# Gated linear attention and a bilinear feed-forward on one core: the values term of chunks 2 to 5 in 128x32 tiles, tokens ordered at y's eviction, and a new order of the whole program

## The chip, the core and the metric

The kernel runs on one core of one Trainium2 chip. The metric is the device time of one execution in microseconds. Of a core's engines five appear here: TensorE (PE, with PEld for its weight loads), VectorE (DVE), ScalarE (ACT), GpSimd (POOL) and SyncE (SP, which here only issues DMAs). DMAs issued by SP and ACT go through hardware queues (q1 in the profile), those issued by POOL through a software queue (q0); only the latter convert types on the way here.

## The reference

Inputs are q, k, v, alpha of shape (4, 8, 768, 48), that is batch, head, token and head dimension, and three weight matrices. All are float32, and so is the output.

```python
state = np.zeros((B, H, D, D))
for t in range(S):
    state = alpha[:, :, t, :, None] * state + np.einsum('bhd,bhe->bhde', k[:, :, t], v[:, :, t])
    y[:, :, t] = np.einsum('bhd,bhde->bhe', q[:, :, t], state)
x = y.transpose(0, 2, 1, 3).reshape(B * S, H * D)      # 3072 tokens x 384
return (x @ w_a) * (x @ w_b) @ w_out                    # d_ff = 1536
```

The recurrence is computed in blocks. With beta the running product of alpha inside a block, the output is a masked product (beta q)(k / beta)^T times v for the tokens of the same block, plus beta q times the state carried into it.

## The kernel before, in words

**Chunks.** The 3072 tokens are six chunks of 512: chunk c takes two batches (u = 0, 1) and 256 tokens of each; c // 2 says which third of the sequence and c % 2 which batches. A chunk's tokens of one batch lie as 128 pairs on the 128 partitions, the rank (0 or 1) of a token in its pair being a free dimension (`load`, L549: "b h (p r) d"). The 128 pairs are two groups g of 64 partitions, and each group is a block of the recurrence with its own state update.

**Steps of a chunk**, by their letters in the program and their lines: `ld` loads q, k, v, a (L549; v becomes bfloat16 on the way); `ln` logarithms (L556, ACT); `l2`, `l2s`, `R`, `AQ` and others form running sums (L564 to L638); `ra`, `lv` bring the first token of each pair to its pair's level (L645 ACT, L652 POOL or DVE); `E` exponentials beta and 1/beta (L667, ACT); `mq`, `mk` multiply them into q and k, which go to the tile QKp (L678, DVE); `dr`, `dl` carry the decay of a block through DRAM into the tile bl (L684, L689, SP); QKp is transposed to kqT by TensorE in chunks 0 and 1 (`C`, `Ce`, L736) and by a DMA in chunks 2 to 5 (`T`, L767, SP); `v` copies the values into a padded tile vx with 96 columns per head, 48 of them zero (L785 ACT, L787 DVE); `K`, `K2` are the state update's matmuls (L799, L812), `k` its DVE part (L826 to L830).

`D` are the scores (L841): 64x64 tiles, four at a time, keys of group g on output partitions g\*64 to g\*64+63, the key's rank in the free dimension. They are masked on the way out of PSUM (`M`, L846, DVE), or copied by ACT and masked in place (`Mc` L850, `Mm` L854). y^T is then summed in PSUM: `SB` and `SA` are the carried terms (a state as weights, the queries as moving data), `Y` the values term (vx as weights, the masked scores as moving data). All three go through one helper, `out_mm` (L865), in 64x64 tiles, and the 64-column zero-padded slices of vx let a 48-wide head straddle two tiles.

`Y` has, for each u, 12 rounds of four 64x64 matmuls (3 slices, 2 ranks, 2 column tiles, 2 groups with the row half). Each multiplies 64 keys. `X` copies y^T, 128x768, from PSUM to xT (L900 ACT, L902 DVE), tokens still in the order group, rank, pair.

**Feed-forward.** `a`, `b` (L919) are three 128x128 by 512 matmuls (256 for half a chunk) per block f of d_ff; `as` copies a out of PSUM (L925, ACT), `pr` multiplies it with b into the tile prod (L933, DVE), and puts the tokens in order as it writes. `o` (L941) multiplies prod with w_out, 128 tokens at a time, `ot` evicts (L956 ACT, L958 DVE), `st` stores (L974, SP). `oc`, `otc`, `stc` are the same in column halves at the very end. `W` and `Wo` load the weights through POOL's queue.

**Order.** Nothing reorders: the text `PROGRAM` lists the operations, each engine takes its own in that order, and each engine waits at its next operation until the data is there. So a late transfer stalls the engine that reads it, with all that it has listed behind. The operations' letters are mapped to functions in the table `OPS` (L995 to L1062). A number at the end of `D`, `a`, `o` and others is the PSUM bank.

Of the kernel before, what the change touches and what calls it, by code (L numbers as in the profile page):

```python
# [65 lines left out]
1: v 0 S; lv 1 q V; mk 0 V
0: pr 10 *
1: mq 1 V; C 0 1 4
0: as 9 *
1: C 0 0 2  # L70
0: o 0 0 5; pr 7 *
1: dk * 6
2: ld k * P
3: ld v * P
0: cz 1 v P; pr 9 *
1: Ce 0 0 S; E 1 i; de *; lv 1 k P; Ce 0 1 V; D 0 1 1; D 0 0 3
0: pr 3 1
1: Mc 0 0; K2 0 0 7 0
0: o 1 0 6
1: mk 1 V; M 0 1  # L80
0: o 3 0 4; o 1 1 -; ot 1 S; c3 P
3: ld a * P
0: cs 1 0 P; o 3 1 -
1: k 0 0 V; k 0 1 V; Mm 0 0 V; SB 0 1; C 1 0 3; C 1 1 7
0: ot 3 S; o 0 1 -
1: Ce 1 0 V
2: ln *
1: v 1 V; D 1 0 3; Ce 1 1 S; K2 1 1 6 0; Y 0; SA 0
0: ot 0 V
1: k 1 0 V; D 1 1 6  # L90
0: o 2 0 5
1: M 1 0
2: l2 0 V
1: X 0 S; a 3 0 1; Mc 1 1
2: l2s 0 P; l2s 1 P
1: a 2 0 3; a 4 0 4
2: R 0
1: k 1 1 V; as 4 0
2: ra 1
1: as 3 0; b 4 0 7  # L100
0: o 2 1 -
1: as 2 0
0: ot 2 S
1: pr 4 0
2: R 1; lv 1 q P
1: b 3 0 6; b 2 0 7; a 5 0 2; pr 3 0; b 5 0 3; as 5 0; b 1 0 5; a 1 0 1; pr 5 0; pr 2 0; a 7 0 2; as 1 0; pr 1 0
2: AQ 3
1: SB 1 6
2: lv 0 k P
1: a 10 0 5  # L110
2: lv 1 k V; ra 0; ld v * P
1: Mm 1 1 V
2: E 1 b
1: as 10 0; b 10 0 0; pr 10 0
2: mq 1 V; E 1 i
1: as 7 0; b 7 0 1
2: E 0 b; E 0 i
1: a 0 0 5
0: st 3 Y
2: dr  # L120
1: SA 1; Y 1
2: mk 1 V
1: pr 7 0; a 11 0 0; a 6 0 3; b 6 0 2; X 1 S; b 11 0 4; a 2 1 6; as 6 0; a 3 1 7; as 11 0; b 2 1 1; pr 6 0
2: lv 0 q V
1: b 4 1 0; as 2 1
2: T 1
1: pr 11 0
2: dl
0: st 0 Y
1: a 0 1 2; pr 2 1  # L130
2: mq 0 V
1: b 3 1 3; b 0 0 6; as 3 1; as 0 0; b 0 1 7; pr 3 1; a 8 0 1; a 9 0 5
0: st 1 Y
1: b 8 0 3; b 9 0 4; pr 0 0; as 0 1
2: mk 0 V
1: a 4 1 2
3: ln *
1: a 9 1 6; pr 0 1; as 8 0; b 9 1 1
3: ra 1
1: b 10 1 7; pr 8 0; a 10 1 3; as 4 1; as 9 0; as 9 1; a 6 1 6; b 6 1 2; b 11 1 5; pr 4 1; as 10 1; pr 9 0; a 11 1 4; pr 10 1; pr 9 1; as 6 1  # L140
2: v 1 S
1: a 8 1 3; b 8 1 1; a 7 1 6; pr 6 1
3: l2 0 V
1: as 11 1
2: T 0
1: as 8 1; a 5 1 4
3: ra 0
1: as 5 1; a 1 1 2
2: v 0 V
4: ld a * Y  # L150
1: pr 11 1; as 7 1; pr 8 1
2: K2 * * 0 7; D 1 1 3; D 1 0 5
1: as 1 1; b 5 1 2; o 2 0 1
2: k * 0 V
1: pr 5 1
3: v 0 S; v 1 S
1: b 1 1 2
2: Mc 1 0; M 1 1
3: l2s 0 P; l2s 1 P
1: b 7 1 0; o 2 1 -; pr 1 1; o 3 0 4  # L160
2: SB 0 5
1: pr 7 1
3: R 0
2: D 0 0 2
1: ot 2 V
2: Mm 1 0 V
1: o 3 1 -
2: Mc 0 0; SB 1 0; D 0 1 2
3: R 1
1: ot 3 S  # L170
2: SA 0
1: o 0 0 4
0: cs 0 0 P
2: Mc 0 1
4: ln *
3: ld q * Y; ld k * Y
2: k * 1 V
3: AQ 2
2: Y 1; SA 1; Mm 0 1 V; Mm 0 0 V; Y 0; X 0 S
3: E 0 b  # L180
4: l2 0 V
2: X 1 V
1: o 0 1 -
2: b 1 * 6; a 1 * 5
3: E 1 b
4: ld k * Y
3: E 1 i
1: ot 0 S
3: E 0 i
4: l2s 0 P  # L190
2: a 0 * 0; b 0 * 1; as 0 *; as 1 *
3: lv 0 k P; lv 0 q P
2: a 5 * 7
1: st 3 Y
2: a 7 * 4
4: l2s 1 P
2: a 2 * 5
3: lv 1 q V; mq 1 V; lv 1 k V
2: pr 1 *
3: dr  # L200
2: pr 0 *
3: mk 0 V
4: ld q * Y
0: st 2 Y
2: as 5 *; a 6 * 6; b 6 * 2; as 7 *
3: mq 0 V
2: b 9 * 4; b 7 * 0
1: st 2 Y
3: dl
# [6 lines left out]
4: ra 0
2: pr 5 *; a 11 * 6
3: mk 1 V
2: as 9 *; a 3 * 0
4: lv 0 k V; lv 0 q V; R 1  # L220
2: as 2 *
1: o 1 1 -
2: as 11 *; a 8 * 5; b 11 * 2; a 4 * 7; b 2 * 1
3: T 1
1: ot 1 V
2: pr 9 *; as 8 *; pr 11 *; pr 2 *; b 8 * 3; b 4 * 5; as 4 *
5: ld a * Y
3: K2 * * 4 6
2: pr 8 *; as 3 *; pr 4 *
3: k * 0 V; D 0 0 2; Mc 0 0  # L230
2: b 3 * 1
4: ra 1
2: pr 3 *; b 10 * 5; a 10 * 0
3: D 1 0 1; D 1 1 3
2: as 10 *
3: k * 1 V; Mc 1 1
2: o 0 0 7; o 2 0 0
3: M 1 0
5: ln *
2: pr 10 *  # L240
4: lv 1 q P
3: SB 1 3; D 0 1 1; Mc 0 1
4: lv 1 k P
5: ld q * Y
1: st 0 Y
3: SB 0 5
2: o 2 1 -
3: Mm 1 1 V; Mm 0 0 V; Mm 0 1 V
4: ld v * P
2: ot 2 S; o 0 1 -  # L250
4: AQ 0; E 0 b; E 0 i
3: SA 0; Y 0; SA 1
4: E 1 b
3: Y 1
5: l2s 1 V
4: mq 0 V; mk 0 V
3: X 0 S; X 1 S
2: o 3 0 2; o 3 1 -
4: T 0
3: a 5 * 3  # L260
4: E 1 i; v 0 S
3: a 9 * 0
2: ot 3 S
3: b 5 * 6; a 6 * 5; as 5 *
2: st 2 Y
3: as 9 *
5: ld k * P; l2s 0 P
3: as 6 *
5: ra 1
4: mq 1 V  # L270
2: ot 0 S
3: a 0 * 1
4: mk 1 V
3: a 1 * 2
4: D 0 0 3
5: l2 0 V
1: st 1 Y
4: dr
5: R 0
3: pr 5 *  # L280
4: v 1 S; M 0 0
3: b 1 * 7; as 1 *; a 3 * 5; b 9 * 6; pr 9 *; b 6 * 4; a 2 * 0; pr 6 *
4: T 1
5: lv 0 k P
3: b 0 * 6; as 0 *; as 2 *
4: dl
3: a 8 * 1
5: lv 1 q P
3: b 4 * 0; a 4 * 4; b 2 * 3; pr 1 *; pr 0 *; as 8 *; pr 2 *; as 4 *; pr 4 *; b 3 * 6; b 8 * 2
5: ld v * P; lv 1 k P  # L290
3: a 11 * 1
5: ra 0
3: as 3 *; pr 8 *; as 11 *; a 7 * 0
4: D 1 0 3; K * 0 5
5: lv 0 q P
3: pr 3 *; as 7 *
5: v 1 V
# [801 lines left out]
```

## Time and profile before

| | |
|---|---|
| median of 3 runs | 194.11 us (193.99 to 194.12) |
| profiled execution's span | 192.0 us (192.04) |
| PE busy | 186.8 us, 97% |
| PEld busy | 116.9 us, 61% |
| DVE busy | 133.1 us, 69% |
| ACT busy | 106.5 us, 55% |
| POOL busy | 56.9 us, 30% |
| q0, software queue | 18432 packets, 13.37 MB, 39.6% of 16 engines' span |
| q1, hardware queue | 44016 packets, 15.55 MB, 38.1% |

The profile records one execution, and its span stands for that execution's own time; the run's time has some 2 us more around it. Matmuls are pipelined, so the time of a matmul of a group (217 ns for a 64x64) is its latency and not its cost: cost is read from the distance between starts. Several groups of one line overlap in the timeline for the same reason. A DMA's time at its issuing engine is the issue; the landing comes later and is told in us from issue to landing. The 40 slices are 4.8 us each.

### The profile page before, as it was taken

The numbers are of one execution on the slowest core, as the hardware profiler recorded it, in microseconds if no ns is written. First come the engines' busy times: TensorE is split into PE (matmuls) and PEld (weight loads), VectorE is DVE, ScalarE is ACT, GpSimd is POOL, SyncE is SP. The second block draws the span as 40 slices with busy tenths as digits, with TensorE's granted clock in tenths as the row PEclk, the third lists the DMA queues.
The fourth block names the chain that finished last, engine by engine and source line by source line (L and its number), as shares of the span: only waits on it lengthen the run. The fifth ranks groups of instructions, "written<-read, shape, count | busy, mean of one in ns | idle before, by whom it ended". The sixth has DMA issues, their size and how long they took to land.

```text
span 192.0 us, 6086 instructions
## 1 busy us (share of the span) xinstructions
PE 186.8 (97%) x2613; PEld 116.9 (61%) x2613; DVE 133.1 (69%) x223; ACT 106.5 (55%) x194; POOL 56.9 (30%) x75
## 2 busy tenths in 40 slices
PE   7999999999999999999999999999999999999992
PEld 3888875677778876645557444656465644545562
DVE  2387698994989888899897956887567446252510
ACT  4448885656779867753487756743572435314211
POOL 8999626752450500640074262000000000000000
PEclk9999999999999999999999999999999999999999
DMA  5999999999969999999999989017641200000422
GB/s 132 274 219 218 251 253 235 244 269 264 251 107 166 165 216 265 248 254 149 233 213 181 156 174 129 3 42 140 146 66 44 85 0 0 0 0 3 164 82 82
DMA packets 62618, 29.40 MB, mean 153 GB/s; under 512 B 53712, under 2 KB 60768, under 8 KB 62592
## 3 DMA queue, kind: packets, MB, share of 16 engines
q0 software_dynamic: 18432, 13.37, 39.6%
q1 hardware_dynamic: 44016, 15.55, 38.1%
q8 instruction: 20, 0.33, 0.7%
q10 hardware_dynamic: 144, 0.10, 0.2%
q14 instruction: 6, 0.05, 0.1%
HBM read 25.98 MB, written 4.74 MB: 160 GB/s over the span
## 4 chain that ended last, share of the span: by engine, by line
PE 91%; DMA 5%; SPq 1%; DVE 1%; issue 1%; ACT 0%; DVEq 0%
PE psum L919 47%; PE psum L941 24%; PE psum L865 7%; PE psum L841 3%; DMA kqT<-QKp 3%; DMA q_t<-in_q_dram 3%; PE psum L736 2%; PE psum L633 1%; PE psum L952 1%; SPq L549 1%; PE psum L799 1%; PE psum L812 1%; PE psum L700 1%; PE psum L591 1%; PE psum L592 1%
## 5 line engine op out<-in xcount | busy, mean ns | idle before, releaser
L919 PE MATMUL psum<-xT,wb_t 128*128 128x512 bf16 (+1 forms) x270 | 56.0, 337 | 0.0
L919 PE MATMUL psum<-xT,wa_t 128*128 128x512 bf16 (+1 forms) x270 | 56.0, 337 | 0.0
L941 PE MATMUL psum<-wo_t,prod 128*128 128x384 bf16 x276 | 49.4, 326 | 0.0
L919 PEld LDWEIGHTS <-wb_t 128*128 128x128 bf16 x270 | 25.9, 98 | 19.9 <-issue 0.5
L919 PEld LDWEIGHTS <-wa_t 128*128 128x128 bf16 x270 | 25.9, 98 | 19.7 <-issue 0.3
L941 PEld LDWEIGHTS <-prod 128*128 128x128 bf16 x276 | 25.9, 98 | 17.6
L956 ACT ACTIVATE ot<-psum 128x384 f32<-128x384 f32 (+1 forms) x16 | 7.7, 482 | 22.7 <-PE psum L941 21.6
L850 ACT ACTIVATE m<-psum 128x1024 bf16<-128x1024 f32 x14 | 14.1, 1023 | 4.6 <-PE psum L841 4.3
L613 POOL TENSOR_TENSOR l<-la 64x384 f32<-64x384 f32 x7 | 7.8, 1108 | 26.6 <-ACT la L556 19.0
L846 DVE TENSOR_TENSOR m<-psum,mask 128x1024 bf16<-128x1024 f32 x10 | 12.1, 1220 | 3.1 <-PE psum L841 3.1
L652 POOL TENSOR_TENSOR q_t<-q_t,ra 128x384 f32<-128x384 f32 x5 | 6.1, 1215 | 22.5 <-ACT ra L645 19.7
L556 ACT ACTIVATE la<-a_t 128x1536 f32<-128x1536 f32 (+2 forms) x9 | 9.5, 1055 | 2.3 <-DMA a_t<-in_alpha_dram 2.2
L678 DVE TENSOR_TENSOR QKp<-q_t,beta 128x768 bf16<-128x768 f32 x10 | 10.0, 995 | 1.0 <-ACT beta L667 1.0
L865 PE MATMUL psum<-m,vx 64*64 64x128 bf16 x576 | 10.5, 217 | 0.0
L900 ACT ACTIVATE xT<-psum 128x768 bf16<-128x768 f32 x9 | 7.2, 816 | 5.7 <-PE psum L865 5.5
L678 DVE TENSOR_TENSOR QKp<-k_t,invb 128x768 bf16<-128x768 f32 x10 | 9.7, 972 | 0.8 <-ACT invb L667 0.8
L854 DVE TENSOR_TENSOR m<-m,mask 128x1024 bf16<-128x1024 bf16 x14 | 9.3, 684 | 1.2 <-ACT m L850 1.2
L958 DVE COPY ot<-psum 128x384 f32<-128x384 f32 (+1 forms) x9 | 4.8, 532 | 7.6 <-PE psum L941 4.7
L865 PEld LDWEIGHTS <-vx 64*64 64x64 bf16 x576 | 9.0, 107 | 0.5 <-issue 0.3
L841 PE MATMUL psum<-kqT 64*64 64x128 bf16 x384 | 9.0, 219 | 0.4 <-DMA kqT<-QKp 0.3
L652 POOL TENSOR_TENSOR k_t<-k_t,a_t 128x384 f32<-128x384 f32 x6 | 7.4, 1228 | 6.1 <-issue 3.3
L549 POOL DMA_DIRECT2D v_t<-in_v_dram x8 | 8.5, 1058 | 0.1
(271 smaller groups left out, 287.9 us busy)
## 6 DMA issues: line engine op xcount, KB each, us to landing
out_dram<-ot SPq DMA_DIRECT2D x23, 192.0 KB, 3.8
q_t<-in_q_dram SPq DMA_DIRECT2D x3, 768.0 KB, 6.5
a_t<-in_alpha_dram POOLq DMA_DIRECT2D x2, 768.0 KB, 15.2
k_t<-in_k_dram POOLq DMA_DIRECT2D x2, 768.0 KB, 12.1
v_t<-in_v_dram POOLq DMA_DIRECT2D x4, 384.0 KB, 7.0
a_t<-in_alpha_dram SPq DMA_DIRECT2D x2, 768.0 KB
k_t<-in_k_dram SPq DMA_DIRECT2D x2, 768.0 KB
a_t<-in_alpha_dram POOLq DMA_DIRECT2D x3, 384.0 KB, 8.5
```

Of the source, the lines that this page charges most:

```text
L549: eng.dma_start(out=t[:, us, hs].rearrange("p b h r d -> p (b h) (r d)"), in_=src[ch.b0 + us.start:ch.b0 + us.stop, hs, ch.s * 2 * C:(ch.s ...
L556: nc.scalar.activation(out=ch.la[:, us, hs].rearrange("p b h r d -> p (b h r d)"), in_=ch.a[:, us, hs].rearrange("p b h r d -> p (b h r d) ...
L613: eng.tensor_add(ch.l2[(1 - g) * HC:(2 - g) * HC, 1], x[:, :, 0, :], x[:, :, 1, :])
L652: eng.tensor_mul(x, x, by)
L678: eng.tensor_mul(QKp[ch.c % 2][:, u, j, :, hs, :D], src[:, u, hs].rearrange("p h r d -> p r h d"), f)
L841: nc.tensor.matmul(s2[g * HC:(g + 1) * HC, r, p, rk, :], lhsT=turned_part(ch, u, 1, rk, 2 * h + p, g, rs), rhs=queriesT(ch, u, 2 * h + p, ...
L846: nc.vector.tensor_mul(m.rearrange("p r a k s -> p (r a) (k s)"), ch.s2[u, h].rearrange("p r a k s -> p (r a) (k s)"), maskn(4))
L850: nc.scalar.activation(out=m.rearrange("p r a k s -> p (r a) (k s)"), in_=ch.s2[u, h].rearrange("p r a k s -> p (r a) (k s)"), func=AF.Copy)
L854: eng.tensor_mul(x, x, maskn(4))
L865: nc.tensor.matmul(y[c * DP:(c + 1) * DP, g, j // 2 * C:(j // 2 + 1) * C], lhsT=lhsT, rhs=rhs, start=(g, c) not in begun, stop=False, skip ...
L919: nc.tensor.matmul(p, lhsT=(wa_t, wb_t)[w][:, kk, f * 128:(f + 1) * 128], rhs=ch.xT[:, kk, us, :], start=(kk == 0), stop=(kk == KT - 1))
L941: nc.tensor.matmul(op, lhsT=ch.prod[:, f, at:at + C], rhs=wo_t[:, f, :], start=(f == 0), stop=(f == NFF - 1))
```

## The change

- For chunks 2 to 5 (`NR = 2`) the masked scores keep the key's rank on the partition half and the group in the free dimension, so that a block of 128 keys lies on 128 partitions. The values term then uses weight tiles of 128 rows by 32 columns, four column tiles, 32 matmuls per u instead of 48 (`inner_rows`). A mask for that layout is made by two POOL copies (`cm2`), and the scores' loops go in another order.
- The weights of that term need the values with a group's 64 pairs split by rank over the partitions. Four new DMAs per chunk (`lw`, `load_rows`) bring them from DRAM on POOL's queue into a tile that shares its space with vx, 72 columns per head, 24 of them zeroed (`cz w`). The copy `v` goes away in these chunks; the state update reads v_t directly.
- y is evicted per group, 128x384 at a time (24 evictions instead of 12), and this eviction writes the tokens in order, in all chunks. xT is laid out by 128-token group, and `pr` writes prod without reordering.
- The keys of chunk 5 load on SP's queue instead of POOL's. The whole PROGRAM is placed anew.

```diff
+    VP = D + DP // 2
+    NR = 2
+    mask2 = cst.tile([C, 2, HC], BF16, name="mask2")
+    vps = [t.rearrange("p b r h e -> p (b r h e)")[:, :4 * H * VP].rearrange("p (g b h e) -> p g b h e", g=2, b=2, h=H) for t in vxs]
...
+    def const_mask2(eng):
+        for rk in range(2):
+            ks = slice(rk * HC, (rk + 1) * HC)
+            ENG[eng].tensor_copy(mask2[ks], mask[ks, rk])
...
+    def load_rows(ch, g, rk, eng):
+        at = ch.s * 2 * C + g * C
+        eng.dma_start(out=vps[ch.c % 2][rk * HC:(rk + 1) * HC, g, :, :, :D].rearrange("p b h d -> p (b h) d"),
+                      in_=v[ch.b0:ch.b0 + 2, :, at:at + C, :].rearrange("b h (s r) d -> r s (b h) d", r=2)[rk])
...
+    def values(ch, gs, u, rk, hd):
+        return ch.v[gs, u, hd, rk, :] if ch.c >= NR else vxs[ch.c % 2][gs, u, rk, hd, :D]
...
     def scores(ch, u, h, tag):
...
-            for rk in range(2):
-                for g in range(2):
+            for x in range(2):
+                for y in range(2):
                     for r in range(2):
+                        rk, g = (y, x) if ch.c >= NR else (x, y)
                         rs = slice(r * DP, (r + 1) * DP)
-                        nc.tensor.matmul(s2[g * HC:(g + 1) * HC, r, p, rk, :], lhsT=turned_part(ch, u, 1, rk, 2 * h + p, g, rs),
+                        half, part_ = (rk, g) if ch.c >= NR else (g, rk)
+                        nc.tensor.matmul(s2[half * HC:(half + 1) * HC, r, p, part_, :], lhsT=turned_part(ch, u, 1, rk, 2 * h + p, g, rs),
                                          rhs=queriesT(ch, u, 2 * h + p, g, rs), start=True, stop=True)
...
+    SLICES = [(h, 3 * (h // 2) + j) for h in range(H) for j in ((0, 1) if h % 2 == 0 else (1, 2))]
+    RANKS = [[x for x in SLICES if x[1] % 4 == c] for c in range(4)]
+
+    def inner_rows(ch, u):
+        y, begun = ch.y[u]
+        vp = vps[ch.c % 2].rearrange("p g b h e -> p g b (h e)")
+        W32 = DP // 2
+        for n in reversed(range(len(SLICES) // 4)):
+            for g in range(2):
+                for c in range(4):
+                    h, j = RANKS[c][n]
+                    at = h * VP + W32 * j - D * h
+                    nc.tensor.matmul(y[c * W32:(c + 1) * W32, g, j // 4 * C:(j // 4 + 1) * C], lhsT=vp[:, g, u, at:at + W32],
+                                     rhs=ch.m[u, h // 4][:, h % 2, h // 2 % 2, g, :], start=False, stop=False, skip_group_check=True)
...
-    def evac(ch, u, eng):
+    def evac(ch, u, g, eng):
         if not hasattr(ch, "xT"):
-            ch.xT = wk.tile([128, KT, B, C], BF16, name="xT")
-        o_ = ch.xT[:, :, 2 * u:2 * u + 2, :].rearrange("p a g s -> p g a s")
-        i_ = ch.y[u][0][:, :, :KT * C].rearrange("p g (a s) -> p g a s", a=KT)
...
+            ch.xT = wk.tile([128, B, KT, C], BF16, name="xT")
+        evict(ch.xT[:, 2 * u + g].rearrange("p a (s r) -> p a r s", r=2),
+              ch.y[u][0][:, g, :KT * C].rearrange("p (a r s) -> p a r s", a=KT, r=2), eng)
...
-        o_, a_, b_ = tokens(ch.prod[:, f, :], us), columns(a[:, :n], n), columns(b, n)
-        nc.vector.tensor_mul(o_, a_, b_)
+        nc.vector.tensor_mul(ch.prod[:, f, us.start * C:us.stop * C], a[:, :n], b)
```

Of the new PROGRAM, the first feed-forward operations, the stretch around the transposes of chunk 2, and that around the transposes of chunk 4:

```
0: C 1 1 2; X 0 1 V; cz 1 q P; D 1 0 6; Mc 1 0; Ce 1 1 V; W a 0 256; W b 256 768; K 1 0 5; de 1; k 1 0 V; b 0 0 0; cs 1 m P
...
0: a 0 0 1; as 0 0; a 1 0 2; as 1 0; pr 0 0; b 1 0 3; pr 1 0; a 2 0 4; as 2 0; ...
...
2: lv 1 k V; ld v * P
1: b 11 0 6
2: mq 1 V
1: b 1 0 0; Y 1
0: cz 0 w P
1: pr 3 0
2: dr; mk 1 V; T 1
1: SA 1; X 1 0 V; X 1 1 S; a 1 0 4; as 1 0; a 5 0 1; a 7 0 5; b 7 0 3; as 5 0; b 5 0 4; pr 1 0
0: cm2 P
2: dl
1: a 11 0 2; b 6 1 0; a 6 1 1; as 7 0; pr 7 0; a 3 1 3; as 11 0; pr 5 0
2: lw 0 0 P; mk 0 V
1: b 0 1 2; b 6 0 4; a 0 1 5; as 6 1; pr 6 1; pr 11 0; as 6 0
2: lw 0 1 P; ra 0; lw 1 0 P; lw 1 1 P
0: cz 1 w P
1: pr 6 0; a 9 1 0; a 8 1 1; a 4 1 4; as 0 1; b 4 1 5
3: lw 0 0 P
1: b 9 1 6
2: lv 0 q V
1: a 9 0 7; pr 0 1
3: lw 0 1 P
2: mq 0 V
1: b 3 1 2
3: lw 1 0 P
1: as 9 1; pr 9 1
3: ln *
1: as 3 1; pr 3 1; as 4 1; pr 4 1; a 10 1 0; as 10 1; b 10 1 6; b 10 0 3; a 10 0 2; pr 10 1; as 10 0
3: lw 1 1 P
1: as 9 0
2: D 1 0 4; Mc 1 0
...
4: E 0 i; mk 0 V; E 1 b; lw 1 0 P; lw 1 1 P
2: o 1 0 2; o 1 1 -; ot 1 S
4: mq 0 V; T 0
2: o 3 0 1
5: l2s 1 V
2: o 3 1 -; ot 3 S
4: dr; mq 1 V; mk 1 V
3: a 2 * 2; b 2 * 0; a 1 * 1; as 2 *
4: T 1; dl
3: as 1 *; b 1 * 2
...
5: AQ 6; E 0 b; ld v * P
4: D 0 0 4
3: pr 5 *
5: lw 0 0 P; E 0 i
...
```

More of the change, by code (lines that the diff above doesn't have):

```diff
@@ L216 @@
[L216 to L242, printed above, removed]
+1: b 1 1 1; pr 1 1; o 2 1 -
```

631 lines of the change are left out of this document (288 added, 343 removed).

## The prediction

> **What bounds the kernel now.** I read the page's busy shares first, then its 40 slices, then the chain that ended last, and then the matmuls in order of time around the places that the diff touches.
>
> ```profile
> span 192.0 us, 6086 instructions
> PE 186.8 (97%) x2613; PEld 116.9 (61%) x2613; DVE 133.1 (69%) x223; ACT 106.5 (55%) x194; POOL 56.9 (30%) x75
> PE   7999999999999999999999999999999999999992
> PEclk9999999999999999999999999999999999999999
> DMA  5999999999969999999999989017641200000422
> PE 91%; DMA 5%; SPq 1%; DVE 1%; issue 1%; ACT 0%; DVEq 0%
> ```
>
> TensorE is busy for 97%, at full granted clock, and carries 91% of the chain: time that it saves is time saved, and any wait of TensorE is added to the end. The row to keep in mind is DMA: its engines are full through the first 24 slices (115 us), though nothing waits for them. The waits of TensorE say so:
>
> ```profile
> PE psum L574 <- DVE og L472: 1.2, 1, 1.2
> PE psum L841 <- DMA kqT<-QKp: 0.3, 1, 0.3
> PE psum L736 <- DVE QKp L678: 0.2, 1, 0.2
> ```
>
> One DMA wait in the whole span, 0.3 us, for a transpose. Before and after these lines TensorE's starts are at their usual pitch. So two questions decide: what the new values term saves on TensorE, and whether 16 more loads keep the DMA hidden. The profiled execution spans 192.04 us, the median of the runs is 194.11, so 2.07 us lie around the span and are taken as unchanged.
>
> **The change part by part.** *Values term (Y).* The matmuls of it before:
>
> ```profile
> L865 PE MATMUL psum<-m,vx 64*64 64x128 bf16 x576 | 10.5, 217 | 0.0
> 129.01 0.87 PE L865 MATMUL psum<-m,vx 64*64 64x128 bf16 x48
> 129.71 0.22 PE L865 MATMUL psum<-kqT,S 64*64 64x128 bf16 x1
> ```
>
> 48 matmuls go from 129.01 to 129.71: four 64x64 tiles run at once, so 12 rounds of 58 ns; over the blocks at 76.32, 103.59 and 129.87 a round is 56 to 59, I take 56. The eight blocks of chunks 2 to 5 have 96 rounds. After, a block has 32 matmuls of 128x32 with the same 128 moving columns, four column tiles: 8 rounds, 64 in all. If a round still lasts 56 ns: 32 x 56 = -1.79 us. No row has 128x32 tiles. The bound below is that value (the 128 columns are the same); the bound above is two tiles at a time, 64 x 112 against 96 x 56 = +1.79. The nearest row is the state update of chunk 5, whose matmuls keep to one row half and alternate between two column tiles:
>
> ```profile
> 140.97 0.62 PE L799 MATMUL psum<-vx,QKp 64*64 64x48 bf16 x28
> 141.40 0.25 PE L841 MATMUL psum<-kqT 64*64 64x128 bf16 x2
> ```
>
> 28 in 0.43 us, 31 ns a pair, with a new weight load each: column tiles on the same rows do overlap, loads included, so I take 56. [...]
>
> *Tile-mode changes.* Where the tile shape changes, the next matmul starts 93 ns late: 309 against 216 ns after a 128x512, 255 against 163 after a 128x384, 203 against 110 after a 128x256 (start to start). Y used to stand in one 64x64 run with the carried terms (129.71 above); now it is a run of its own. Walking the two programs operation by operation gives 55 changes before, 64 after: +9 x 93 = +0.84. TensorE's work together: -1.79 + 0.84 = -0.95 us.
>
> *Evictions, casts, products.* Nine y evictions of 816 ns on ACT and three of 952 on DVE become 13 on ACT and 11 on DVE of half the size, nearest rows 482 and 532 ns for 128x384: +2.0 us together. Eight of twelve value casts go (six of 850 on ACT, two of 350 on DVE): -5.8. Products (0.72 us at 512) and masks keep their sizes. ACT at 55% and DVE at 69% hide all of it in TensorE's 97%; the new stride-2 write of the eviction has no row, and between nothing and twice 482 ns it would add to ACT and DVE at most 12 us that idle time covers, save at a chunk's turn, where TensorE waits for the first eviction: there a half eviction is ready 0.3 us sooner. I count 0. The memsets and two mask copies on POOL (30% busy) are 0 for the same reason; they delay what POOL issues behind them by well under 2 us.
>
> *Start.* The new order begins the feed-forward with b 0, a 0, a 1, the old with a 4, a 3. Weights land at 14.39 (b, first 256 columns), 17.41 (a, 256 to 768), 18.48 (a, first 256), 20.43 (b, 256 to 768). Before, the first of these matmuls starts at 18.32 in weights that have been there for 0.9 us. After, a 0 cannot start before 18.48 and b 2 not before 20.43. Bounds 0 (other work fills it) to +0.6; I take +0.3. At the end the last stores issue from SP instead of ACT, 1.74 against 1.66 us to landing: +-0.1, 0.
>
> *Keys of chunk 5.* Their load leaves POOL's queue (issue 100.57, 1.17 us, landed 107.93) for SP's, behind q of chunk 5, ahead of stores and the transposes of chunk 4. An issue on SP took 0.4 to 3.8 us (72.87), and SP issued nothing from 97.2 to 106.47: 0, unless SP is then still behind.
>
> *The new loads.* Each of chunks 2 to 5 gets four row loads on POOL's queue, each 1024 descriptors of 96 bytes written. Queued behind each other, a v load of 2048 lands 2.6 us after the k load before it (52.98, 50.40). Half of it is 1.3 us, an estimate from that row; 16 x 1.3 = 20.6 us of all DMA engines. Eight of the sixteen (10.4 us) are issued in one stretch with v of chunks 2 and 3, from about 50 to 62 us, where DMA is full, and four beside v of chunk 4 and of chunk 5. What such a pairing costs is in the trace of before:
>
> ```profile
> 112.00 3.27 SPq L767 DMA_TRANSPOSE kqT<-QKp  x1
> 112.04 1.19 POOL L549 DMA_DIRECT2D v_t<-in_v_dram  x1
> v_t<-in_v_dram POOLq DMA_DIRECT2D x1, 384.0 KB, 8.1
> DMA to landing us min/median/max: 4.3/5.1/5.9
> ```
>
> Transposes take 4.3 to 5.9 us to land by the last line; it leaves this one out, which was issued in one moment with a v load: its last increment is at 120.0, 8.0 after its issue, and the v load takes 8.1 instead of 5.7. It waits for the other queue's burst. [...]
>
> Who waits: scores (L841) for the transposes. *Chunk 2, u 1:* from the transpose's place to the first scores the new list has 23 half groups of 3 x 110 ns, the carried terms and mode changes: 8.1 us. DVE has 5.5 us of work ahead of the multiplication that the transpose reads, against 3.6 of TensorE's, so it is issued up to 1.9 late: room 6.2 to 8.1, I take 6.7 as DVE's list ahead of that is full too (the old room was 9.4: 58.46 to the scores at 67.86). With a landing of 4.4 (58.46 to 62.90 now) the cost is 0. With 8.0 it is 1.3. With eight row loads ahead it could be 4.4 + 3.6 + 8 x 1.3 = 18, cost 11. I take 1.3: the nearest row by what runs beside it. *Chunk 4, u 1:* 11 groups of 0.65, scores and state: 8.4 us, less 1.2 that SP is held by the transpose before (3.03) and the decay rows (1.20): 7.2. It stands beside v of chunk 5 as in the row above: 8.0 - 7.2 = +0.8; bounds 0 and, with four row loads in front, +6. *Chunks 3 and 5* have rooms of 5 to 8 us with no row loads at that time: 0 each. The decay loads, 4.6 to 5.0 beside a v load against 2.4 to 3.0, hold DVE's state update in chunk 2 (bl L689); DVE's slack covers 0.5 to 2 us: 0.
>
> *The sum:* 192.04 - 0.95 + 0.3 + 1.3 + 0.8 = 193.49, and 2.07 around it: 195.56, that is 195.6 us, slower by 1.4.
>
> **The rivals.** *B, the DMA stays hidden, faster.* One condition: the transposes of chunks 2 and 4 land within 6.7 and 7.2 us of issue. For: three of the five transposes issued by 106.5, while DMA is full, land in 4.4 to 5.0 us. Against: the 8.0 row, and the longer burst. 192.04 - 0.95 + 0.3 + 2.07 = 193.46, from 193.1 to 193.7. From 0.3 us of transpose wait in all it is within the noise, from 1.1 slower.
>
> *C, the loads of chunk 3 come late too.* Here they already arrive just in time:
>
> ```profile
> 79.86 1.65 POOL L652 TENSOR_TENSOR k_t<-k_t,a_t 128x384 f32<-128x384 f32 x1 [1.36 <-DMA k_t<-in_k_dram]
> ```
>
> a of chunk 4, q and k of chunk 3 and k of chunk 4 land at 72.94, 76.82, 79.70 and 82.38, 3 us apart: the rate of full engines. If the 10.4 us of row loads go ahead of them, k of chunk 3 lands at some 90, and the chain from it to its landed transposes, now 79.70 to 91.20, ends at 101.6, where the scores come at about 97: +4.6 on top of B's sum and of 1.3: 199.4, range 197.5 to 202.
>
> *D, column tiles do not run four at a time.* Rounds of 112 ns: +1.79 instead of -1.79, with A's waits partly absorbed by the later TensorE: 193.46 + 3.58 = 197.0 up to 199.1.
>
> **How the numbers follow.** A (195.6; own range 194.5 to 197.5) 0.48, B 0.32, C 0.14, D 0.06. A change of 0.2% (0.39 us) is about what a measurement of this kernel can tell from none; the edge between A and B, 193.7 to 194.5, takes 0.06 as "same", out of both. So faster 0.31, same 0.06, slower 0.63. The range 193.1 to 199.4 leaves out a little of B below and half of C above.
>
> **What would show it.** Right: Y blocks of some 0.45 us for 32 matmuls; TensorE's waits list scores waiting for kqT in chunk 2 (about 64 us) and chunk 4 (about 118), together near 2 us; transposes of 8 us to landing; q0's packets near 34,800. Wrong: no such wait (B); state or scores of chunk 3 waiting from 95 us on for many us (C); Y blocks of 0.9 us (D). If the eviction with the stride costs ACT far above 482 ns, the chunk turns would show waits for xT, which I priced at nothing.

## The result, and the profile after

The changed kernel takes 203.24 us (median of 4 runs), the kernel before 194.12 beside it. Two of the four, 204.88 and one of 482.68 us, were slow executions, so the ratio is taken from the other two, 201.52 and 201.59: 3.9% slower, ratio 1.0388 (95% interval 1.0369 to 1.0408). On another chip, later, the ratio was 1.044 (1.0388 to 1.0491). The forecast was 195.6, from 193.1 to 199.4: the sign was right and the size was not. The profiled execution took 201.59 us for a span of 199.5, so 2.1 lie around it as before; in spans the change cost 7.4 us.

The lines of the page that answer to those shown of before:

```profile
span 199.5 us, 5849 instructions
PE 188.4 (94%) x2485; PEld 116.3 (58%) x2485; DVE 130.3 (65%) x223; ACT 104.4 (52%) x198; POOL 68.7 (34%) x94
PE   7999999999997499899999999979999999999993
PEclk9999999999999799999999999999999999999999
DMA  6999999999999999979999979965712200000323
PE 79%; DMA 15%; SPq 3%; issue 1%; DVE 1%; ACT 0%; DVEq 0%
```

TensorE now has holes: slices 12 and 13, counted from 0 (60 to 70 us), and 26 (about 130). In slice 13 its granted clock dips too. DMA's share of the chain went from 5 to 15%. DMA work did not only grow (81,113 packets, 62,618 before), it stays dense longer. The list of TensorE's waits names the holes:

```profile
PE psum L819 <- DMA kqT<-QKp: 4.1, 2, 3.9
PE psum L819 <- DVE prod L920: 1.4, 1, 1.4
PE psum L876 <- issue: 0.7, 1, 0.7
```

The first hole in order of time (TensorE, then the queues of SP and POOL around it):

```profile
63.04 0.49 PE L907 MATMUL psum<-xT,wa_t 128*128 128x256 bf16 x3
67.42 0.64 PE L819 MATMUL psum<-kqT 64*64 64x128 bf16 x16 [3.89 <-DMA kqT<-QKp]
67.85 1.06 PE L788 MATMUL psum<-v_t,QKp 64*64 64x48 bf16 x64
```

```profile
56.86 4.32 SPq L740 DMA_TRANSPOSE kqT<-QKp  x1
```

```profile
53.12 1.19 POOL L517 DMA_DIRECT2D v_t<-in_v_dram  x1
55.92 3.27 POOL L522 DMA_DIRECT2D vx<-in_v_dram  x4
60.05 3.26 POOL L522 DMA_DIRECT2D vx<-in_v_dram  x4 [0.30 <-POOL vx L477]
```

The transpose of chunk 2 was issued at 56.86, the scores could have begun at 63.46 (a room of 6.6 us), and it landed at 67.38, 10.5 us after its issue, among a v load and eight row loads. In the kernel before it landed at 62.90, 4.4 us after its issue, and the scores started in step (run before, SP and TensorE):

```profile
58.46 1.89 SPq L767 DMA_TRANSPOSE kqT<-QKp  x1
67.86 0.63 PE L841 MATMUL psum<-kqT 64*64 64x128 bf16 x32
```

The packets by queue in the changed kernel from 64.3 to 67.4 us, the last 3.1 us of the wait:

```profile
q0 software_dynamic: 2769, 0.26, 193.5%
q1 hardware_dynamic: 1128, 0.01, 64.7%
```

The columns are packets, MB and time as a share of 16 engines. A transpose is 0.52 MB, 2048 packets of 256 bytes; in these 3.1 us the hardware queue moved 0.01 MB in 1128 packets. Nearly all of them have 4 bytes: they are the elements of the two decay loads that SP issued behind the transpose, at 61.36 (3.0 KB each). The transpose's own last data packet began at 64.69, and its sixteen completion increments came from 65.42 to 67.38. So the lateness has two parts. The data took 7.8 us from the issue, and their completion 2.7 us more. In the run without row loads (`no_rows`, below) the same two are 4.2 and 0.5 us. In the 2.7 us of the changed kernel the software queue moved 2,273 packets (0.22 MB) of the row loads. Chunk 4's second transpose in the kernel before, issued at 112.00 beside a v load, has the second part too: its last data packet ended at 116.45, its increments came from 118.73 to 120.0, and between the two the software queue moved 1,781 packets (0.34 MB) of v. The trace does not say which engine carried a packet, so what held a completion back is not shown.

Where the 7.4 us are, from starts against their usual pitch: the transpose wait 3.96; matmuls at a low clock behind it 1.10; a values term that stands at 81.5, 0.82 (the profile names nothing that it waited for, its last mask was done at 81.03, and `after_again` does not have this wait); scores around 123 to 127, 0.68; scores waiting for DVE at 129.7, 1.46; chunk 5's transposes at 144.6, 0.29. Together 8.3, less 0.95 that TensorE's own work became shorter and 0.36 for the wait of before that is gone: 7.0. The remaining 0.4 is not assigned.

### The profile page after: what moved, and what is told of

Its sections match the earlier page's. It is cut to its first block, busy times and chain, and to the rows that moved or that the text cites. A ratio compares the mean times of both kernels' runs of the same rounds, so it can differ in the third digit from the quotient of the medians.

```text
span 199.5 us, 5849 instructions
## 1 busy us (share of the span) xinstructions
PE 188.4 (94%) x2485; PEld 116.3 (58%) x2485; DVE 130.3 (65%) x223; ACT 104.4 (52%) x198; POOL 68.7 (34%) x94
## 2 busy tenths in 40 slices
DMA packets 81113, 30.96 MB, mean 155 GB/s; under 512 B 72400, under 2 KB 79456, under 8 KB 81088
## 4 chain that ended last, share of the span: by engine, by line
PE 79%; DMA 15%; SPq 3%; issue 1%; DVE 1%; ACT 0%; DVEq 0%
PE psum L907 40%; PE psum L928 22%; DMA kqT<-QKp 8%; PE psum L845 4%; DMA bl<-row 4%; PE psum L819 3%; DMA q_t<-in_q_dram 3%; PE psum L876 2%; PE psum L709 2%; SPq L517 1%; PE psum L788 1%; PE psum L939 1%; PE psum L606 1%; PE psum L673 1%; PE psum L564 1%
## 5 line engine op out<-in xcount | busy, mean ns | idle before, releaser
L907 PE MATMUL psum<-xT,wb_t 128*128 128x512 bf16 (+1 forms) x270 | 57.5, 338 | 0.0
L907 PE MATMUL psum<-xT,wa_t 128*128 128x512 bf16 (+1 forms) x270 | 57.3, 339 | 0.0
L943 ACT ACTIVATE ot<-psum 128x384 f32<-128x384 f32 (+1 forms) x21 | 9.9, 479 | 22.9 <-PE psum L928 22.3
L819 PE MATMUL psum<-kqT 64*64 64x128 bf16 x384 | 9.8, 223 | 5.9 <-DMA kqT<-QKp 4.1
L522 POOL DMA_DIRECT2D vx<-in_v_dram x16 | 13.1, 842 | 0.3 <-POOL vx L477 0.3
L625 POOL TENSOR_TENSOR q_t<-q_t,ra 128x384 f32<-128x384 f32 x5 | 5.0, 1006 | 21.4 <-ACT ra L618 21.4
L819 PEld LDWEIGHTS <-kqT 64*64 64x64 bf16 x384 | 6.7, 108 | 9.4 <-DMA kqT<-QKp 4.7
L945 DVE CAST xT<-psum 128x384 bf16<-128x384 f32 x11 | 6.1, 582 | 6.6 <-PE psum L845 4.8
L943 ACT ACTIVATE xT<-psum 128x384 bf16<-128x384 f32 x13 | 7.4, 601 | 3.5 <-PE psum L845 1.8
L625 POOL TENSOR_TENSOR k_t<-k_t,a_t 128x384 f32<-128x384 f32 x6 | 6.5, 1076 | 4.1 <-DMA k_t<-in_k_dram 4.0
```

The costliest lines, as they stand in the source:

```text
L522: eng.dma_start(out=vps[ch.c % 2][rk * HC:(rk + 1) * HC, g, :, :, :D].rearrange("p b h d -> p (b h) d"), in_=v[ch.b0:ch.b0 + 2, :, at:at + ...
L625: eng.tensor_mul(x, x, by)
L819: nc.tensor.matmul(s2[half * HC:(half + 1) * HC, r, p, part_, :], lhsT=turned_part(ch, u, 1, rk, 2 * h + p, g, rs), rhs=queriesT(ch, u, 2 ...
L907: nc.tensor.matmul(p, lhsT=(wa_t, wb_t)[w][:, kk, f * 128:(f + 1) * 128], rhs=ch.xT[:, us, kk, :], start=(kk == 0), stop=(kk == KT - 1))
L943: nc.scalar.activation(out=o_, in_=i_, func=AF.Copy)
```

## The experiments

Two theories stood at first. One: the row loads hold back the completions of transposes and decay loads. The other: the new order itself leaves too little room. All ratios are to the kernel before, in runs on the same chip; the chip is not the same in all rows, so rows are compared by their ratios.

| run | median us | ratio (95%) |
|---|---|---|
| no_rows | 195.48 | 1.0076 (1.0038 to 1.0115) |
| late5 | 200.43 | 1.0294 (1.0244 to 1.0343) |
| before_rows | 202.89 | 1.0458 (1.0399 to 1.0516) |
| gated | 202.22 | 1.0385 (1.0340 to 1.0429) |
| warm | 205.12 | none given |
| late5_warm | 200.49 | 1.0314 (1.0272 to 1.0355) |
| tile45 | 194.15 | 1.0005 (0.9989 to 1.0022) |
| tile45b | 194.53 | 1.0030 (1.0007 to 1.0054) |
| tile45c | 193.60 | 0.9983 (0.9965 to 1.0000) |
| keys5 | 194.97 | 1.0045 (1.0027 to 1.0062) |
| keys5_apart | 194.63 | 1.0036 (1.0016 to 1.0056) |
| after_again | 202.61 | 1.0440 (1.0388 to 1.0491) |
| no_rows_apart | 194.72 | 1.0017 (0.9977 to 1.0057) |
| order64 | 203.84 | 1.0386 (1.0336 to 1.0436) |
| order64b | 199.32 | 1.0230 (1.0160 to 1.0300) |

### The row loads left out, and the row loads alone

`no_rows` is the changed kernel without its sixteen `lw`, so its values term multiplies whatever lies in the tile:

```diff
-2: lw 0 0 P; mk 0 V
+2: mk 0 V
...
```

> The changed kernel with the sixteen row loads left out (the weights of the values term are then whatever lies in the tile, so the values term of chunks 2 to 5 is wrong; every other instruction stays). Theory 'the row loads hold back the completions of the transposes and decay loads': the 3.9 us wait at 63.5 goes, with the 1.1 us of low clock behind it, and the waits of 0.9 us at 81.5 and 2.3 us around 123 to 131; the time is that of the other terms, 193.5 us (193.0 to 194.1). Rival 'the new order has too short rooms whatever the loads do': it stays above 199 us. Rival 'half and half': 196 to 198.

Measured: 195.48 us, ratio 1.0076. Against the ratio of 1.0388 the loads cost 3.1%, 6.0 us. The first transpose of chunk 2 lands 4.7 us after its issue (56.97 to 61.65) and its wait is gone. But the time is 2 us above the forecast of 193.5, and slower than before: something else is lost too (below).

`before_rows` is the converse: the old order, with the same loads added into a tile that nothing reads.

```diff
-2: lv 1 k V; ra 0; ld v * P
+2: lv 1 k V; ra 0; ld v * P; lw 0 0 P; lw 0 1 P; lw 1 0 P; lw 1 1 P
+3: lw 0 0 P; lw 0 1 P; lw 1 0 P; lw 1 1 P
...
-4: ld v * P
+4: ld v * P; lw 0 0 P; lw 0 1 P; lw 1 0 P; lw 1 1 P
...
-5: ld v * P; lv 1 k P
+5: ld v * P; lw 0 0 P; lw 0 1 P; lw 1 0 P; lw 1 1 P; lv 1 k P
```

> The kernel before, with the sixteen row loads added behind its own v loads (eight behind v of chunk 2, four behind that of chunk 4, four behind that of chunk 5), into a tile that nothing reads; nothing else changed. Theory 'the loads do it, in any order with such rooms': transposes of chunk 2 land 9 to 12 us after issue, k of chunk 3 at 84 to 90, slower by 3 to 8 us: 197 to 202. Rival 'only the new order makes them hurt': 194.1 to 194.8.

202.89 us, 4.6% slower and 0.9 us above the range: the loads alone, in an order of which no other line was touched, cost as much as the whole change. The transposes of chunk 2 land 10.0 and 8.0 us after issue, k of chunk 3 at 86.1. The places are others than in the changed kernel: TensorE's longest wait is for a transpose of chunk 4, and the next comes by way of DVE, which stands for a decay load of chunk 2. TensorE's waits by its profile, and the two rows:

```profile
PE psum L848 <- DMA kqT<-QKp: 3.1, 2, 2.7
PE psum L926 <- DVE prod L940: 1.9, 1, 1.9
118.27 0.42 PE L848 MATMUL psum<-kqT 64*64 64x128 bf16 x16 [2.67 <-DMA kqT<-QKp]
72.25 0.56 DVE L837 TENSOR_TENSOR Sm<-tmp,bl 128x384 bf16<-128x384 f32 x1 [2.81 <-DMA bl<-row]
```

The first theory holds, and it does not need the new order. Nor is it completions alone that are late: in the changed kernel the transpose's data took 7.8 us for the 4.2 of no_rows, their completion 2.7 for 0.5.

### The loads at other times

`late5` moves v and the row loads of chunk 5 behind the landing of chunk 4's second transpose, by a POOL copy of one element that reads it (`gatet`):

```diff
-5: AQ 6; E 0 b; ld v * P
+5: AQ 6; E 0 b
...
 5: lv 1 k P
+4: gatet 1
+5: ld v * P; lw 0 0 P; lw 0 1 P; lw 1 0 P; lw 1 1 P
```

> The changed kernel with v of chunk 5 and the four row loads of chunk 5 issued behind the landing of chunk 4's second transpose (POOL waits for it), not beside it. Theory: that transpose lands 4.3 to 5 us after its issue instead of 7.6, the decay loads in 2.4 to 3.5 instead of 7.5, and DVE's 2.5 us wait for bl goes: the 2.3 us around 123 to 131 are saved, 199.2 (198.8 to 199.8). Rival 'those waits come from DVE being behind since chunk 2': 201.2 to 201.6.

The transpose lands 4.45 us after its issue instead of 7.64, the decay loads after 2.3 to 2.95 instead of 7.5, and the wait of 1.46 us at 129.7 is gone, as the theory has it. The total, 200.43, is above its range of 198.8 to 199.8; the ratio is 1.0294 where the change had 1.0388 and 1.044. That wait had come to TensorE by way of DVE, which stood in its state update with all its later work behind it (changed kernel, DVE):

```profile
126.99 0.55 DVE L805 TENSOR_TENSOR tmp<-psum,S 128x384 f32<-128x384 f32 x1
130.00 0.56 DVE L806 TENSOR_TENSOR Sm<-tmp,bl 128x384 bf16<-128x384 f32 x1 [2.46 <-DMA bl<-row]
```

`gated` moves the loads of chunks 2 and 3 too:

```diff
-3: ld v * P
+2: ld v * P
...
-2: lw 0 0 P; mk 0 V
+2: mk 0 V; gatet 1; lw 0 0 P; lw 0 1 P; lw 1 0 P; lw 1 1 P
...
-3: ld q * Y; ld k * Y; lv 0 k P
+3: ld q * Y; ld k * Y; lv 0 k P; ld v * P; lw 0 0 P; lw 0 1 P; lw 1 0 P; lw 1 1 P
```

> The changed kernel with all its loads, at other times: v of chunk 2 takes the early place of v of chunk 3 in POOL's queue, so that the queue is empty when chunk 2's first transpose is issued; chunk 2's row loads are issued once that transpose has landed, v and the row loads of chunk 3 once k of chunk 3 has landed, those of chunk 5 once chunk 4's second transpose has landed. Theory 'it is when they are issued, since a transpose waits for the other queue's bursts': chunk 2's first transpose lands 4.4 to 5 us after issue, the waits of 3.9, 1.1 and 2.3 us are gone, the time is that of the kernel without row loads or up to 1.5 us more: 194 to 196.5. Rival 'it is their volume, whenever they come': another transpose or load comes late instead, 198 or more.

202.22: the rival's range holds. Chunk 2's transpose, with POOL's queue empty, lands in 4.4 us (59.48 to 63.87), and chunk 4's in 4.5. But those of chunk 3 now meet the moved loads. SP takes 5.7 us to issue the first of them (2.2 in the changed kernel), the second goes out at 97.99 and lands 6.0 later, and the wait is back there, longer (TensorE, run gated):

```profile
97.01 0.69 PE L783 MATMUL psum<-v_t,QKp 64*64 64x48 bf16 x64
104.07 0.64 PE L814 MATMUL psum<-kqT 64*64 64x128 bf16 x16 [6.36 <-DMA kqT<-QKp]
```

The profiled execution is the longest of the four (207.6 us, the others 200.7 to 202.9), so its 6.4 us is the high end. At the two places tried, the DMA engines had no room for eight row loads: moving them moved the wait. Whether fewer and larger descriptors for the same rows would cost less was not tried.

### The clock behind a long wait

In the changed kernel, after TensorE had stood for 3.9 us (4.2 from start to start), 128x256 matmuls started 213 ns apart instead of 110. The granted clock by stretches, run late5 (the columns that matter: stretch, its length, TensorE's busy time, and PEclk, the third from the end), and then run late5_warm:

```profile
66.00:68.90 2.90, 0.00 (x0) 0.00 (x0) 0.00 (x0) 0.00 (x0) 0.00 (x0) 0.95 2.64 80
68.90:72.00 3.10, 3.04 (x88) 2.56 (x89) 1.38 (x3) 1.71 (x3) 0.00 (x0) 0.50 1.51 169
```

```profile
66.00:71.00 5.00, 4.95 (x40) 2.41 (x43) 0.83 (x3) 0.66 (x2) 1.52 (x3) 1.00 2.27 116
71.00:74.00 3.00, 3.00 (x100) 2.73 (x90) 2.05 (x4) 2.00 (x4) 0.00 (x0) 1.00 0.79 186
```

`warm` and `late5_warm` (on late5, with 20 in place of 17) put idle matmuls into the wait:

```diff
-1: as 9 0
+1: as 9 0; fill 17 4
 2: D 1 0 4; Mc 1 0
```

> The changed kernel with 17 idle matmuls of 128x512 (3.7 us, on data that nothing reads) put ahead of the scores of chunk 2, so that TensorE works through the wait for the transpose. Theory 'an idle TensorE of 3.9 us loses its granted clock, and that is a term of its own': the transpose still lands near 67.4, the scores start at the same time, and the matmuls behind them run at 110 instead of 213 ns: 1.1 us or a little more less, about 200.4. Rival 'the slow matmuls have another cause (weights or moving data late)': 201.5 to 201.7, no change.

> The changed kernel with chunk 5's loads late (as in the run before that did this alone), and 20 idle matmuls of 128x512 (4.3 us, on data that nothing reads) ahead of chunk 2's first scores, while the transpose is under way. Theory 'after the idle wait TensorE runs at a lower granted clock, and that costs 1 to 2 us': granted clock 1.0 throughout, 198.0 to 198.9 in every run where the run without them had 198.5 to 200.7. Rival 'the loss has another cause': 200.4.

By their totals both miss: warm has a median of 205.12, and in its profile chunk 4's second transpose took 10.4 us and TensorE waited 3.4 for it, and late5_warm has 200.49 where 198.0 to 198.9 was expected. In the profiles the mechanism is there in both: behind the idle matmuls the clock stands at 1.00 and the 128x256 matmuls start 110 ns apart; in warm it falls to 0.50 behind its other wait, the 3.4 us.

What the low clock costs can be estimated from late5 and late5_warm. In late5_warm the 20 matmuls last 4.3 us and ran on for 2.1 us after the transpose had landed (68.62, scores at 70.75), since TensorE reached them 1.9 us later than in late5. About 1 us of that delay is half clock in the start, where "1.0 throughout" had been expected (run late5_warm):

```profile
11.20:14.60 3.40, 3.40 (x30) 3.16 (x20) 2.23 (x2) 0.23 (x1) 3.40 (x6) 0.50 1.48 195
```

The rest are short waits at 24, 42 and 50 us. From the first scores to the last matmul late5_warm takes 124.63 us, late5 126.42: 1.8 less, of which some 0.5 is a wait at 143.5 that late5 alone has. So the low clock costs about 1.3 us, an estimate from one profile of each; the pitch in the changed kernel gave 1.10. No total shows it.

### What the new order loses without the row loads

In no_rows TensorE waits 1.46 us at 116.5 for a step of chunk 5's sums on DVE. That DVE step and POOL beside it (run no_rows):

```profile
113.86 2.52 DVE L588 TENSOR_TENSOR lh<-l 128x768 f32<-128x768 f32 x1
116.42 1.64 DVE L588 TENSOR_TENSOR ll<-lh 128x768 f32<-128x768 f32 x1
```

```profile
113.23 1.22 POOL L509 DMA_DIRECT2D v_t<-in_v_dram  x1
114.46 1.01 POOL L617 TENSOR_TENSOR k_t<-k_t,a_t 128x384 f32<-128x384 f32 x1
115.43 1.81 POOL L617 TENSOR_TENSOR q_t<-q_t,ra 128x384 f32<-128x384 f32 x1
```

Elsewhere the same DVE instruction takes 0.95 us and the same POOL instruction 1.00. `no_rows_apart` holds POOL's work until chunk 4's second transpose has landed, when DVE is done:

```diff
-5: l2s 0 P; lv 0 k P
+5: l2s 0 P
...
-5: ra 1; lv 1 q P
+5: ra 1
...
-5: AQ 6; E 0 b; ld v * P
+5: AQ 6; E 0 b
+4: gatet 1
+5: lv 0 k P; lv 1 q P; ld v * P
```

> The run without row loads (values term of chunks 2 to 5 on whatever lies in the tile), with POOL's multiplications of chunk 5's keys and queries and its v load held until chunk 4's second transpose has landed, so that POOL is idle while DVE splits chunk 5's sums (L588). Without this those two DVE instructions took 2.52 and 1.64 us, and TensorE waited 1.46 us for the second. Theory 'POOL and DVE hold each other up': both take 0.95 us, the 1.46 us wait goes, 1 to 2 us less than without: 193.3 to 194.5. Rival 'DVE is late for other reasons': the wait stays above 1 us, 195 or more.

Both take 0.96 us and TensorE's wait is gone:

```profile
115.45 0.96 DVE L590 TENSOR_TENSOR lh<-l 128x768 f32<-128x768 f32 x1
116.44 0.96 DVE L590 TENSOR_TENSOR ll<-lh 128x768 f32<-128x768 f32 x1
```

So POOL and DVE held each other up in no_rows: DVE's two took 4.16 us where apart they take 1.92, and POOL's two 2.82 where twice 1.00 is usual. At 0.95 and 1.00 us each, the two of DVE and the two of POOL would take 3.9 us one after another, and they take 4.2 (113.86 to 118.06). What the two engines share is not shown.

The median of 194.72 is above the expected range, but the runs divide: the five at a granted clock of 0.998 or more took 193.29 to 194.44, four of them 193.6 or less (the forecast of the rival without DMA trouble was 193.46), the others at 0.990 or 0.991 took 195.0 to 196.8. In no_rows the six at full clock have a median of 194.84 where before had 194.28 on that chip; here the five have 193.40 where it had 193.87. So the gain is 1.0 us in runs at full clock, a comparison chosen after the result. The profiled run is one of those at the lower clock, and its clock stands at 0.50 from 11.6 to 15.0 us, in the start, before any of this. Why the new order's start loses the clock in some executions was not tried.

`order64` and `order64b` are the new order with the old tiles, no row loads, and the value copies back (the copies as order64b has them):

```diff
-    NR = 2
+    NR = 9
...
+2: v 1 S; v 0 V
...
+3: v * S
```

> The changed kernel with neither the 128x32 tiles nor the row loads: new order, y's eviction per group and in token order, keys of chunk 5 on SP; the values term of all chunks in 64x64 tiles as before, the value copies of chunks 2 to 5 on DVE ahead of their state updates (and chunk 5's values term a little later). Theory: what the run without row loads had over the forecast of 193.5 (195.5 was measured) comes from the new order's own waits, so this is that run plus the tiles' 0.95 us: 195.5 to 197. Rival 'the tiles themselves cost what the run without row loads lost': 194 to 194.6.

> As the run with new order, 64x64 tiles and no row loads, its value copies now earlier (on ACT for chunks 3 to 5, on ACT and DVE for chunk 2), ahead of the state updates by some matmuls. Theory: the 5.1 us of TensorE waits for these copies go, and what is left is the run without row loads plus the tiles' 0.95 us: 195 to 197.5. Rival 'the new order without tiles is worth as much': 194 to 195.

Both are above every range. order64 (203.84) says little: I had put the copies right ahead of the state updates, and TensorE waited 5.1 us for them. With the copies earlier order64b is still 2.3% slower than before, its waits (0.2 to 0.4 us each, at 42, 50, 66, 84 and 122 to 126) spread over ACT and DVE; the profiled execution also has half clock in its start, 12.0 to 15.3. By the ratios it is 1.5% above no_rows, 3.0 us, of which 0.95 is TensorE's longer work. So in these two placements the new order without the tiles has no worth of its own. How much of the 2.0 us that no_rows loses against the forecast is the order, and how much the clock in the start, stays open.

`after_again` is the changed kernel once more, on the chip of the last two.

> The changed kernel, unaltered, on the chip of the next two runs: 201 to 205 us.

202.61, with the same waits: 4.5 us for chunk 2's transpose (landed 11.2 us after issue), 1.4 at 129.7.

### One part alone: the keys of chunk 5

`keys5` changes one load of the kernel before:

```diff
-5: ld q * Y
+5: ld q * Y; ld k * Y
...
-5: ld k * P; l2s 0 P
+5: l2s 0 P
```

> The kernel before with one part of the change alone: keys of chunk 5 load on SP's queue, behind q of chunk 5, instead of POOL's. In the trace of before they land at 107.93 and chunk 4's first transpose (issue 106.47) at 111.46, for which TensorE waits 0.36 us. Theory: the keys land before 105, the transpose in 4.3 to 4.6, the wait goes: 0.2 to 0.4 us less than before. Rival 'nothing hangs on it': within 0.1 us of before. Rival 'SP's queue is then too full': a store or transpose issues late, slower.

0.45% slower. The keys land at 104.5, 3.4 us sooner. So POOL multiplies them sooner, and does it while DVE prepares chunk 4's first transpose (DVE, then POOL; in each fence run before first, then run keys5):

```profile
105.46 0.95 DVE L678 TENSOR_TENSOR QKp<-k_t,invb 128x768 bf16<-128x768 f32 x1
106.03 1.75 DVE L678 TENSOR_TENSOR QKp<-k_t,invb 128x768 bf16<-128x768 f32 x1
```

```profile
108.06 1.41 POOL L652 TENSOR_TENSOR k_t<-k_t,a_t 128x384 f32<-128x384 f32 x1 [3.34 <-issue]
105.37 1.59 POOL L652 TENSOR_TENSOR k_t<-k_t,a_t 128x384 f32<-128x384 f32 x1
```

The transpose is issued at 107.84 (106.47 before) and TensorE waits 1.35 us for it, where it was 0.36. `keys5_apart` lists POOL's step later:

```diff
-5: lv 0 k P
...
-5: lv 1 q P
+5: lv 1 q P; lv 0 k P
```

> The run with keys of chunk 5 on SP's queue, and POOL's multiplication of those keys (L652) listed behind the multiplication of chunk 5's q, so that it does not run while DVE multiplies chunk 4's keys into the transposes' input. In the run without this, that DVE instruction (L678) took 1.75 us instead of 0.95 beside POOL's, chunk 4's first transpose was issued 0.8 later, and TensorE waited 1.35 us instead of 0.36. Theory 'POOL and DVE hold each other up': the L678 takes 0.95 us, the transpose wait is 0.1 to 0.5 us, the time 193.7 to 194.2, 0.8 to 1.1 less than the run without it. Rival 'the keys' place in SP's queue did it': the wait stays above 1 us, 194.7 or more.

In the profile it is as the theory has it: 0.95 us, and no wait for the transpose (scores at 111.52, in step):

```profile
105.79 0.95 DVE L677 TENSOR_TENSOR QKp<-k_t,invb 128x768 bf16<-128x768 f32 x1
111.52 0.42 PE L840 MATMUL psum<-kqT 64*64 64x128 bf16 x16
```

The total is a miss. The profiled execution took 193.54, but the median of the twelve is 194.63, 0.36% above before. The other eleven have no trace; what they lose is open, and so is how much of keys5's 0.45% came from the two engines side by side.

### One part alone: the tiles, where DMA has room

`tile45` is the kernel before with `inner_rows` in chunks 4 and 5 only, their row loads behind chunk 4's transposes.

```diff
+    NR = 4
...
+4: gatet 1; lw 0 0 P; lw 0 1 P; lw 1 0 P; lw 1 1 P
...
-5: lv 0 q P
+5: lv 0 q P; ld v * P; lw 0 0 P; lw 0 1 P; lw 1 0 P; lw 1 1 P
...
-5: v 1 V
...
-5: v 0 S
```

> The kernel before, its order kept, with the 128x32 tiles alone, and in chunks 4 and 5 alone, where DMA has room: their value copies go, their row loads and v of chunk 5 are issued behind the landing of chunk 4's second transpose. Theory: 16 rounds of 56 ns less and 4 or 5 changes of tile mode of 93 ns more, -0.5 us, and the 0.3 us wait for chunk 4's first transpose stays: 193.4 to 193.9 where before is 194.2, faster by 0.15 to 0.4%. Rival 'the tile gains nothing': 194.2 or more.

No difference. 16 rounds fewer are -0.90, but tile modes change 6 times more often, not 4 or 5 (+0.56), and the memsets and mask copies that I had put ahead of v of chunk 4 made TensorE wait 0.6 us for the transpose instead of 0.36.

`tile45b` and `tile45c` have carried terms ahead of both values terms, 2 more changes of mode than before, and the memsets earlier; tile45b has the keys on SP besides.

```diff
-4: Y 0; SA 0
+4: SA 0; SA 1; Y 0
...
-4: X 0 V; Y 1; SA 1
+4: X 0 V; Y 1
...
-5: SA 1; Y 1
+5: SA 1; SA 0; Y 1
```

> The run with 128x32 tiles in chunks 4 and 5 of the old order, mended twice: the carried terms of both u run ahead of the values terms (2 more changes of tile mode than before, not 6), and keys of chunk 5 on SP's queue. Theory, by the same sum that forecast this kernel's gain: -16 x 56 + 2 x 93 = -0.71 us, and up to 0.36 us of transpose wait less: 0.7 to 1.1 us below before. Rival 'the tile form itself gains nothing': 0 to 0.36 us below before.

> The old order with 128x32 tiles in chunks 4 and 5, carried terms of both u ahead of the values terms, row loads behind chunk 4's transposes, and keys of chunk 5 left on POOL's queue as in the kernel before. Theory: the sum is -16 x 56 + 2 x 93 = -0.71 us, and the transpose wait is back at 0.3 to 0.6 us: 193.2 to 193.6 where before has 194.0, faster by 0.2 to 0.4%. Rival 'the tile form gains nothing': 194.0 or more.

tile45b loses the gain to the keys: a 1.5 us wait for chunk 4's first transpose, as in keys5. tile45c takes 193.60 where before takes 194.05, ratio 0.9983, whose interval ends at 1.0000. That is the upper end of the theory's range, at the edge of what can be told from no change. Its profile bears the sum out: the wait for chunk 4's first transpose was 0.78 instead of 0.36, so -0.71 + 0.42 = -0.29 us, and the span is 0.25 shorter (191.79 for 192.04). The run also drops four value copies and moves loads, so the tiles alone are not told apart. It is the best version here, after two that gained nothing. Its values terms of both u, 64 matmuls, take 1.0 us with the change of mode before them:

```profile
130.11 1.08 PE L922 MATMUL psum<-m,vx 128*32 128x128 bf16 x64
131.12 2.12 PE L985 MATMUL psum<-wo_t,prod 128*128 128x384 bf16 x12
```

## Why the prediction was wrong

The sign and the mechanism were right: row loads hold up transposes, and TensorE waits. The step that failed is the size of the term for chunk 2's transpose, 1.3 us forecast and 3.96 measured, and with it three costs that the sum had at nothing. The profiled span is 6.0 us above the forecast of 193.49: 2.7 by this term, 1.1 by the clock behind the wait, 0.7 by the decay load (1.46 where 0.8 stood for chunk 4's transpose), and 1.8 by the waits at 81.5, 123 to 127 and 144.6; the small rest cancels or is not assigned. Term by term:

- **Values term, right.** In the changed kernel 64 matmuls run from 109.03 to 110.03:

```profile
109.03 1.08 PE L876 MATMUL psum<-m,vx 128*32 128x128 bf16 x64
110.03 0.37 PE L606 MATMUL psum<-l,utb 64*64 64x384 bf16 x4
```

  These are 16 rounds of 57 ns and a mode change. All four column tiles run at once, and rival D is out. The weight loads of these tiles share all rows, and no cost of theirs shows beside the matmuls: a round of the kernel before took 56 to 59 ns.
- **Mode changes, right** in count (both traces have them: 64 against 55) and size (256 ns for 163 from a 128x384 to a 128x32 at 109.03).
- **Chunk 2's transpose, mechanism and place right, size wrong.** The room was 6.6 us (forecast 6.7). The landing was forecast at 8.0, from the row with one v load beside it; it was 10.5 with v and eight row loads, and 8.9 to 11.2 in the five other runs that issue these loads around it. I had put down 18 as its upper end and took the value nearest by kind, though the burst was five times as long by my own estimate (2.6 + 8 x 1.3 = 13 us against 2.6). Cost 3.96 for 1.3. Nor was it a later completion alone: of the 5.8 us by which it lands later than in no_rows, 3.6 are later data and 2.2 a later completion.
- **A term left out: the clock.** A wait of 3.9 us was followed by half the granted clock up to 70.4 us (128x256 matmuls 213 ns apart for 110), 1.1 us more. The forecast priced waits at their length.
- **Chunk 4's transpose, landing right, price misplaced.** 7.6 us after issue (forecast 8.0); its own scores waited 0.3. What cost 1.46 was the decay load of the same moment, which landed 7.5 us after its issue and held DVE for 2.46. The prediction had a decay term for chunk 2 alone, 4.6 to 5.0 us, and put it at nothing because DVE's slack of 0.5 to 2 us would cover it.
- **DVE beside POOL, not thought of.** The prediction let POOL's added and moved steps cost nothing since POOL is 30% busy. They lengthened DVE's (0.95 to 2.52 us in no_rows): with the loads out, the kernel is still 0.8% slower than before instead of 0.3% faster, and keeping the two engines apart brings it to 0.2%. The rest of that is not assigned.
- **Rival C** named the jam, but in the wrong chunk: k of chunk 3 landed at 85.1 and not at 90, and since TensorE was by then 6 us later itself, nothing waited. In gated a jam came in chunk 3, but another: its transposes met the moved loads.
- **Eviction, start, tail: no cost seen.** The eviction with the stride takes 601 ns on ACT and 582 on DVE where 482 and 532 were the nearest rows, and no wait of TensorE for xT shows. TensorE's idle time up to 60 us is 1.6 us in both profiles.

## What to carry to other kernels

Loads that stand behind no listed wait of TensorE were not free here while the DMA engines were full: among the row loads chunk 2's first transpose landed 10.5 us after its issue, without them 4.7. Ask what else is to land in the same stretch, and price such a load by the whole burst, not by one load of it. Here waits of 2.67 and 3.89 us on TensorE cost more than their length (1.10 us more behind the second), and work moved on one of POOL and DVE could be paid on both (in no_rows 2.52 us for 0.95 on DVE, 1.81 for 1.00 on POOL). A saving of 1 us on the bound engine is worth testing alone, in the stretch that has room for what it needs, before an order is built around it.

## What was not expected of the hardware

- The granted clock halved behind a wait: 2.67 us of waiting in before_rows (115.60 to 118.27; 3.05 from start to start) was followed by 427 ns starts for 216 up to 122.0, 1.89 us (71.31 to 73.20) was not.
- It also fell to 0.50 without such a wait: in late5_warm from 11.2 to 14.6 us and in no_rows_apart from 11.6 to 15.0, where TensorE's longest wait since its first matmul had been 0.67 and 0.23 us. What did it is not shown.
- Two instructions of POOL and two of DVE side by side: 2.52 and 1.64 us for 0.95 on DVE, 1.01 and 1.81 for 1.00 on POOL.
- Faster data did not make a faster kernel: keys that landed 3.4 us sooner let POOL's multiplication start 2.7 us sooner, into DVE's, and the median was 0.45% longer; only the profile ties the two together.
